# The third unit's down layer as seven products of matrix quarters

## The chip, the cores and the metric

The kernel runs on one core of one Trainium2 chip. A core has five engines that the text names by the profile's short names: PE (TensorE, matrix products), DVE (VectorE), ACT (ScalarE), POOL (GpSimd) and SP (SyncE, which here only issues transfers). Each engine works through its own list of instructions in order and waits on semaphores for the others. The metric is the device time of one execution in microseconds (us), lower is better. The kernel before was timed at 528.81 us (median of three runs, 528.71 to 529.97).

## The reference

Three stages stand one behind the other: a Nystrom attention over 4 batches of 576 tokens, a dense layer with a gated activation, and a routed layer with 8 experts. Only the last one matters here. For the tokens of one expert it computes

```
h = np.maximum(np.einsum('ecd,edf->ecf', disp, w1), 0.0)
y = np.einsum('ecf,efd->ecd', h, w2)
...
out[i] = gate_w[i] * y[expert_idx[i], pos[i]]
```

with D = 512 features, F = 1024 hidden features, everything in float32. The first product with its ReLU is called the up layer here, the second one with the factor gate_w the down layer.

## The kernel before

The last stage is worked off in *units* of 576 tokens of one expert. For the data at hand each of the batches 0 to 2 is one unit, and `run_unit(i)` (L1181) is called three times; the third is the last work of the program. A float32 product is made of three products of a rounded half and a rest: every operand X is split (`split`, L1051) into hi = round(X), written by ACT, and lo = X - hi, written by DVE or POOL, and PE adds hi*hi + hi*lo + lo*hi in one PSUM bank.

Up layer of the second and third unit (`up_seven`, L1137): the product is already done with seven products of matrix quarters instead of eight (the Winograd form of Strassen's method). For each of four blocks m of 128 hidden features PE makes seven products of 6 matmuls of 288 columns; DVE adds them up from PSUM into the buffers `mix` (lines L1140), and `put_h` (L1077) writes ReLU of the four sums: ACT writes hT[0] (hi, L1079) and the last 64 tokens unsplit to `h_tail` (L1081), DVE writes hT[1] (lo, L1082). The PSUM banks of these products form a ring of six. `split2(f)` (L1074) splits the eight 512-wide slices of w2 on ACT and POOL.

Down layer (`down_layer`, L1155): one call for each tile of 128 tokens. The unit has four full tiles and one of 64 tokens. The loop in `run_unit` begins with the small one (16 matmul passes of L1170 in plain float32, its sum and scale at L1176 to L1178), then come the tiles 3, 2, 1, 0. A full tile is 24 matmuls of 512 columns into one bank (8 slices f of the hidden features, three products each, L1163). ACT scales the finished bank with the gate (L1174) and the tile, 256 KB, is stored by a transfer that SP issues (L1197); the last tile's transfer is issued by ACT.

While unit 0 and 1 are in their down layer, ACT and DVE prepare the quarters and their sums for the next unit's up layer (`prepare_w`, `prepare_x`). The third unit has no successor: in its down layer DVE and ACT have little to do. At the end each engine takes a branch (L1365) past a part of the program that is not needed for this data, and the engines meet (L1442). `redo` (L1200) loads the flag for that branch into registers. Instructions of this part of the program are put in order by a scheduler when the kernel is built, so an engine's list is not the order of the source text.

## Time and profile before

| what | us |
|---|---|
| median of three runs | 528.81 |
| the profiled execution | 529.06 |
| its span, first to last instruction | 527.3 |
| third unit: up layer on PE | 474.32 to 497.0 |
| third unit: 64-token tile on PE | 497.03 to 500.6 |
| third unit: four full tiles on PE | 500.62 to 522.67 |
| last scaling on ACT | 522.75 to 523.44 |
| last store issued | 523.47 |

All times inside the program are counted from the start of the span. A row of the timeline gives the start, the length, the engine, the line, what is written from what, the shape, and after x the number of instructions that follow each other without a gap; its length is from the first start to the last end. Ends of matmuls are modelled. The profiled execution took 1.8 us more than its span and 0.25 us more than the median of the runs.

### The profile page before, as it was taken

How to read it: one execution, taken by the hardware profiler on the slowest of the kernel's cores; microseconds unless marked ns; L12 is line 12 of the kernel's file. 1: busy time of each engine (PE TensorE's matmuls, PEld its weight loads, DVE VectorE, ACT ScalarE, POOL GpSimd, SP SyncE). 2: the span in 40 equal slices, each digit the busy share in tenths (PEclk: the TensorE clock that was granted, in tenths of full speed). 3: DMA queues.
4: the chain of work that ended last, by engine and by line, in shares of the span. 5: the costliest groups of instructions: out<-in, count | busy, mean ns of one | idle time of the engine just before them, and what ended most of it. 6: DMA issues, size and time to landing. Idle time of an engine off the chain costs nothing. (4 is left out here: it accounts for less than half of the span.)

```text
span 527.3 us, 12038 instructions
## 1 busy us (share of the span) xinstructions
PE 515.0 (98%) x4760; PEld 449.2 (85%) x4760; DVE 343.0 (65%) x781; ACT 293.9 (56%) x684; POOL 200.7 (38%) x254
## 2 busy tenths in 40 slices
PE   8898899999999999999999999999999999999996
PEld 6565778988889998988989999999897899689785
DVE  0789988656867876854965353357836958987700
ACT  1868878766867554744644343446346564864411
POOL 2468978987230542212513323323160070016000
PEclk9999999999999999999999999999999999999999
DMA  7896803002735521140120000129621470510011
GB/s 272 307 368 231 283 19 99 30 1 91 229 103 154 177 81 35 48 171 1 45 88 0 1 2 1 67 89 322 253 112 56 159 283 1 179 51 23 2 51 44
DMA packets 24240, 59.72 MB, mean 113 GB/s; under 512 B 2928, under 2 KB 7536, under 8 KB 24176
## 3 DMA queue, kind: packets, MB, share of 16 engines
q1 hardware_dynamic: 23360, 58.60, 31.9%
q8 instruction: 39, 0.64, 0.5%
q10 hardware_dynamic: 816, 0.28, 0.2%
q14 instruction: 25, 0.20, 0.1%
HBM read 45.89 MB, written 12.98 MB: 112 GB/s over the span
## 5 line engine op out<-in xcount | busy, mean ns | idle before, releaser
L433 PE MATMUL py<-ghi,wo 128*128 128x288 f32 x768 | 157.7, 297 | 0.0
L419 POOL TENSOR_TENSOR glo<-r,ghi 128x288 fp32r<-128x288 f32 x88 | 74.5, 849 | 137.7 <-ACT ghi L412 80.3
L433 PEld LDWEIGHTS py<-ghi,wo 128*128 128x128 f32 x768 | 123.2, 188 | 2.6 <-issue 2.0
L389 PE MATMUL ph<-at,vv 128*128 128x288 f32 x768 | 121.6, 299 | 1.0 <-DVE r L402 0.7
L389 PEld LDWEIGHTS ph<-at,vv 128*128 128x128 f32 x768 | 106.6, 188 | 11.2 <-issue 4.3
L433 PE MATMUL py<-glo,wo 128*128 128x288 f32 x384 | 113.5, 296 | 0.0
L400 ACT ACTIVATE r<-ph,half 128x288 f32<-128x288 f32 x128 | 63.5, 500 | 62.3 <-PE ph L389 33.7
L402 DVE SCALAR_TENSOR_TENSOR r<-r,ph 128x288 f32<-128x288 f32 x128 | 56.9, 450 | 48.8 <-ACT r L400 47.9
L433 PEld LDWEIGHTS py<-glo,wo 128*128 128x128 f32 x384 | 72.1, 188 | 0.0
L1163 PE MATMUL ps_o<-w2s,hT 128*128 128x512 f32 x288 | 66.2, 390 | 0.0
L1163 PEld LDWEIGHTS ps_o<-w2s,hT 128*128 128x128 f32 x288 | 53.8, 188 | 13.5 <-issue 2.4
L1053 POOL TENSOR_TENSOR w2s<-wi,w2s 128x512 fp32r<-128x512 f32 x24 | 31.6, 1344 | 87.0 <-ACT w2s L1052 87.0
L412 ACT ACTIVATE ghi<-r 128x288 fp32r<-128x288 f32 x96 | 42.1, 444 | 33.5 <-DVE r L402 33.3
L445 DVE TENSOR_TENSOR yacc<-py,yacc 128x288 f32<-128x288 f32 x72 | 32.7, 454 | 33.9 <-PE py L433 33.8
L1140 DVE TENSOR_TENSOR mix<-ps,mix 128x288 f32<-128x288 f32 x56 | 23.9, 452 | 11.6 <-PE ps L1132 10.9
L276 POOL TENSOR_TENSOR wo<-cvt,wo 128x512 fp32r<-128x512 f32 x16 | 21.0, 1313 | 24.3 <-ACT wo L274 18.9
L1079 ACT ACTIVATE hT<-mix 128x288 fp32r<-128x288 f32 x32 | 13.7, 445 | 26.8 <-DVE mix L1140 26.8
L369 DVE TENSOR_TENSOR vv<-ps_v,vv 128x512 fp32r<-128x512 f32 x32 | 21.8, 686 | 7.0 <-ACT vv L367 6.8
L735 PE MATMUL pn<-yy 128*128 128x96 f32 (+2 forms) x112 | 22.3, 293 | 2.2 <-POOL yy L687 1.5
L735 PEld LDWEIGHTS pn<-yy 128*128 128x128 f32 x112 | 17.1, 189 | 8.0 <-POOL yy L687 2.6
L1174 ACT ACTIVATE rows_o<-ps_o,prob 128x512 f32<-128x512 f32 x12 | 8.3, 689 | 24.0 <-PE ps_o L1163 19.2
L367 ACT ACTIVATE vv<-ps_v 128x512 fp32r<-128x512 f32 x32 | 18.4, 593 | 4.0 <-PE ps_v L362 3.9
(219 smaller groups left out, 831.3 us busy)
## 6 DMA issues: line engine op xcount, KB each, us to landing
raw<-in_moe_w_in SPq DMA_DIRECT2D x16, 512.0 KB, 4.0
raw<-in_moe_w_out SPq DMA_DIRECT2D x16, 512.0 KB, 4.6
wi<-in_moe_w SPq DMA_DIRECT2D x6, 1024.0 KB, 6.5
r_d<-r SPq DMA_DIRECT2D x32, 144.0 KB, 1.9
vm<-in_v SPq DMA_DIRECT2D x8, 512.0 KB, 7.2
raw<-in_moe_w SPq DMA_DIRECT2D x4, 1024.0 KB, 6.3
qT<-in_q SPq DMA_DIRECT2D x6, 576.0 KB, 6.0
qT<-in_k SPq DMA_DIRECT2D x6, 576.0 KB, 7.3
```

The lines of the kernel that those rows point to most:

```text
L369: nc.vector.tensor_tensor(lo[:, b, :], ps[i], hi[:, b, :].bitcast(F32), op=ALU.subtract)
L389: nc.tensor.matmul(ph, lhsT=vv[pair][g][a][:, b, f * P:(f + 1) * P], rhs=at[pair][c][:, g, tok], start=n == 0, stop=n == 3 * NG - 1)
L400: nc.scalar.activation(r, ph, AF.Relu, bias=half, scale=1.0 / 6.0)
L402: nc.vector.scalar_tensor_tensor(r, r, 1.0, ph, op0=ALU.min, op1=ALU.mult)
L412: nc.scalar.activation(ghi, r, AF.Copy)
L419: nc.gpsimd.tensor_tensor(glo, r, ghi.bitcast(F32), op=ALU.subtract)
L433: nc.tensor.matmul(py, lhsT=w[a][:, f, d * P:(d + 1) * P], rhs=gh[f][c], start=f == 0 and n == 0, stop=f == NF - 1 and n == 2)
L445: nc.vector.tensor_tensor(y, py, y, op=ALU.add)
L735: nc.tensor.matmul(pn[:, cols], lhsT=yy[:, 0:P], rhs=yy[:, cols], start=True, stop=True)
L1053: engine.tensor_tensor(dst[1], src, dst[0].bitcast(F32), op=ALU.subtract)
L1140: plus = lambda dst, ps, x: nc.vector.tensor_tensor(dst, ps, x, op=ALU.add)
L1163: nc.tensor.matmul(ps, lhsT=hT[a][:, f, cols], rhs=w2s[c][:, f, :], start=n == 0, stop=n == 3 * FC - 1)
```

## The change

The four full tiles of the third unit, a product of 512 tokens x 1024 by 1024 x 512, are no longer done tile by tile. A new function `down_seven` makes them with the seven products of quarters: with A = h (tokens by hidden features) and B = w2 cut into quarters, A11 B11, A12 B21, S1 T1, S2 T2, S3 T3, S4 B22 and A22 T4, where S1 to S4 and T1 to T4 are sums and differences of quarters. Each quarter product is 256 tokens x 512 x 256, done for two blocks m of 128 tokens: 12 matmuls of 256 columns each.

- `put_h` gets `keep`: in the third unit ACT also writes ReLU(h) unsplit to `h32` (the buffers raw1, free by then), 288 or 224 columns at a time, because the sums S are made from it.
- `sums_before`: POOL makes T1 = B12 - B11 and T2 = B22 - T1, each 128 x 1024.
- In `down_seven` DVE makes S1 to S4, T3 and T4 (128 x 1024 each) and the lo parts of all eight sums, ACT their hi parts; DVE adds the products from PSUM; ACT scales with the gate. A11, A12, A22, B11, B21, B22 use the split parts that exist anyway.
- Rows 0 to 127 and 128 to 255 of the unit are stored whole, rows 256 to 511 in a right and a left half (128 KB each). The very last half is scaled and added by DVE in one instruction and stored by ACT's queue. `flag` is the old code for `redo`, called at another place.

The core of the diff (line numbers of the changed file differ by 4 in the middle of the program, by about 100 at its end):

```
-        def put_h(f, hf, x):
+        def put_h(f, hf, x, keep=False):
...
+            if keep:
+                n = min(HB, full - hf * HB)
+                nc.scalar.activation(h32[f // NF][:, f % NF, hf * HB:hf * HB + n], x[:, 0:n], AF.Relu)
...
+        def sums_before():
+            (b11, b12), (b21, b22) = quarters(*raw2)
+            nc.gpsimd.tensor_tensor(early_sums[0], b12, b11, op=ALU.subtract)
+            nc.gpsimd.tensor_tensor(early_sums[1], b22, early_sums[0], op=ALU.subtract)
...
+        def down_seven(i, put, flag):
...
+            where = dict(S1=a22, T1=t1, S2=a11, T2=t2, S3=a21, T3=b12, S4=a12, T4=b21)
+            sums = dict(S1=(a21, a22, ALU.add), S3=(a11, a21, ALU.subtract), S2=(a22, a11, ALU.subtract),
+                        S4=(a12, a11, ALU.subtract), T3=(b22, b12, ALU.subtract), T4=(b21, t2, ALU.subtract))
...
+            def times(a, b, m, ps):
+                n = 0
+                for f in range(NF):
+                    for x, y in ((0, 0), (0, 1), (1, 0)):
+                        nc.tensor.matmul(ps, lhsT=ops[a][x][:, f, m * P:(m + 1) * P], rhs=ops[b][y][:, f, :],
+                                         start=n == 0, stop=n == 3 * NF - 1)
+                        n += 1
+                return ps
...
+            add("S1")
+            parts_of("S1", "T1")
+            add("S3", "S2")
+            for m in pair:
+                copy(y[m], times("A11", "B11", m, new()))
+            parts_of("S2")
+            for m in pair:
+                plus(v[m], times("A12", "B21", m, new()), y[m])
+                copy(row[m][:, left], v[m], scale=gates[m])
+            parts_of("T2")
+            add("S4", "T3")
+            for m in pair:
+                plus(w[m], times("S1", "T1", m, new()), y[m])
+            parts_of("S3", "T3")
+            add("T4")
+            for m in pair:
+                ps = times("S2", "T2", m, new())
+                plus(u[m], ps, y[m])
+                plus(v[m], ps, w[m])
+            flag()
+            parts_of("S4")
+            for m in pair:
+                ps = times("S3", "T3", m, new())
+                plus(w[m], ps, v[m])
+                plus(u[m], ps, u[m])
+                copy(row[m + 2][:, right], w[m], scale=gates[m + 2])
+                copy(u[m], u[m], scale=gates[m + 2])
+                put(m + 2, row[m + 2], nc.sync, right)
+            parts_of("T4")
+            for m in pair:
+                plus(v[m], times("S4", "B22", m, new()), v[m])
+                copy(row[m][:, right], v[m], scale=gates[m])
+                put(m, row[m], nc.sync)
+            for m in pair:
+                nc.vector.scalar_tensor_tensor(row[m + 2][:, left], times("A22", "T4", m, new()), gates[m + 2], u[m],
+                                               op0=ALU.mult, op1=ALU.add)
+                put(m + 2, row[m + 2], nc.scalar if m else nc.sync, left)
...
-                    hi = up_seven(f)
+                    hi = up_seven(f, not more)
...
+                if not more and f == NF - 1:
+                    sums_before()
...
+                if not more:
+                    down_seven(i, lambda k, ro, engine, c=slice(0, DM): engine.dma_start(out[i * S + k * P:i * S + (k + 1) * P, c], ro[:, c]), flag)
+                    return
```

DVE's list from the last sums of the up layer on, before. The names: mix are the up layer's sums, hT_5659 the lo part of h, rows_o the output of the 64-token tile.

```order
L1140 TENSOR_TENSOR mix_5674<-ps_6821,mix_5674 128x288
L1140 TENSOR_TENSOR mix_5673<-ps_6831,mix_5673 128x288
L1082 SCALAR_TENSOR_TENSOR hT_5659<-mix_5674,hT_5658 128x288
L1082 SCALAR_TENSOR_TENSOR hT_5659<-mix_5673,hT_5658 128x288
L1177 TENSOR_TENSOR rows_o_5662<-ps_o,rows_o_5662 64x512
L1365 COMPARE_AND_BRANCH
```

And the same place in the changed program. Here w1s_5665 is the lo part of T1, raw_5678 (written) S1, wo_119 the lo part of T2, w1s_5664 that of S1, raw_5677 S3 and then S2; mix_5672 <- ps_d is the first sum of a product of the down layer (A12 B21 for m = 0).

```order
L1144 TENSOR_TENSOR mix_5674<-ps_6835,mix_5674 128x288
L1144 TENSOR_TENSOR mix_5673<-ps_6846,mix_5673 128x288
L1054 TENSOR_TENSOR w1s_5665<-rx,w1s_5665 128x4x256
L1083 SCALAR_TENSOR_TENSOR hT_5659<-mix_5674,hT_5658 128x288
L1083 SCALAR_TENSOR_TENSOR hT_5659<-mix_5673,hT_5658 128x288
L1215 TENSOR_TENSOR raw_5678<-raw_5677,raw_5678 128x4x256
L1054 TENSOR_TENSOR wo_119<-rx,wo_119 128x4x256
L1181 TENSOR_TENSOR rows_o_5662<-ps_o,rows_o_5662 64x512
L1054 TENSOR_TENSOR w1s_5664<-raw_5678,w1s_5664 128x4x256
L1215 TENSOR_TENSOR raw_5677<-raw_5677 128x4x256
L1237 TENSOR_TENSOR mix_5672<-ps_d,mix_5669 128x256
L1215 TENSOR_TENSOR raw_5677<-raw_5678,raw_5677 128x4x256
```

DVE's list, which ended behind the 64-token tile, now goes on with 14 instructions of 1024 elements (one of them already ahead of the last two lo parts of h) and 16 of 256. Behind S2 (raw_5677) the order is: the sum of m = 1, S4, lo of S2, T3, two sums, lo of S3, lo of T3, T4, four sums, lo of S4 (w1s_5667), four sums, lo of T4 (vv_124), two sums, and the two last instructions, which scale and add.

PE's list in the changed program, from the third of the seven products on. Here w1s_5665 and w1s_5664 are T1 and S1, wo_119 and w1s_5666 T2 and S2, at_117 and at_118 the hi and lo of T3, wo_120 is S3, w1s_5667 S4, w2s B22.

```order
L1225 MATMUL ps_d<-w1s_5665,w1s_5664 128x256 x24
L1225 MATMUL ps_d<-wo_119,w1s_5666 128x256 x24
L1280 TENSOR_LOAD redo
L1225 MATMUL ps_d<-at_117,wo_120 128x256 x2
L1225 MATMUL ps_d<-w2s_5656,w1s_5667 128x256
L1225 MATMUL ps_d<-w2s_5657,w1s_5667 128x256
L1225 MATMUL ps_d<-w2s_5656,w1s_5667 128x256
L1225 MATMUL ps_d<-w2s_5657,w1s_5667 128x256
L1225 MATMUL ps_d<-at_118,wo_120 128x256
```

Before, 96 matmuls of 128x512 from w2s and hT stood here. Behind these rows follow 21 more of S3 T3, 2 of A22 T4 (vv_123, the hi part of T4), 20 of S4 B22 that begin with the lo part of S4, and 22 of A22 T4 that begin with the lo part of T4 (vv_124).

## Rows read from the trace of the kernel before

**Rows 1.** Page, part 1: busy time, share of the span, instructions.

```profile
PE 515.0 (98%) x4760; PEld 449.2 (85%) x4760; DVE 343.0 (65%) x781; ACT 293.9 (56%) x684; POOL 200.7 (38%) x254
```

**Rows 2.** Third unit's up and down layer: length, busy us (x) by engine, PEclk, DMA.

```profile
474.30:497.00 22.70, 22.70 (x170) 22.50 (x168) 18.02 (x40) 9.97 (x29) 9.00 (x7) 1.00 0.04 14
...
500.60:522.70 22.10, 22.07 (x98) 17.94 (x96) 0.68 (x1) 3.40 (x5) 0.00 (x0) 1.00 0.12 43
```

**Rows 3.** Timeline of the down layer's full tiles and of the end.

```profile
500.62 22.05 PE L1163 MATMUL ps_o<-w2s,hT 128*128 128x512 f32 x96
...
506.39 0.69 ACT L1174 ACTIVATE rows_o<-ps_o,prob 128x512 f32<-128x512 f32 x1 [3.58 <-PE ps_o L1163]
511.83 0.69 ACT L1174 ACTIVATE rows_o<-ps_o,prob 128x512 f32<-128x512 f32 x1 [4.75 <-PE ps_o L1163]
...
522.75 0.69 ACT L1174 ACTIVATE rows_o<-ps_o,prob 128x512 f32<-128x512 f32 x1 [4.75 <-PEq L1365]
523.47 0.37 ACTq L1197 DMA_DIRECT2D out<-rows_o  x1
```

**Rows 4.** Timeline, PE: two neighbouring products of the third up layer.

```profile
485.74 0.96 PE L1132 MATMUL ps<-xw,w1s 128*128 128x288 f32 x6
...
486.54 0.96 PE L1132 MATMUL ps<-at,vv 128*128 128x288 f32 x6
```

**Rows 5.** Timeline, PE: warming matmuls early in the program.

```profile
11.35 0.83 PE L984 MATMUL warm<-ident 128*128 128x256 bf16 x6
```

**Rows 6.** Timeline, DVE: back to back, while the third unit is prepared.

```profile
460.90 1.22 DVE L1112 TENSOR_TENSOR raw<-raw,raw 128x1024 f32<-128x1024 f32 x1
462.03 0.76 DVE L1125 TENSOR_TENSOR w1s<-rx,xw 128x576 fp32r<-128x576 f32 x1
```

**Rows 7.** Timeline, DVE sums from PSUM: four in a row, then two.

```profile
489.00 1.75 DVE L1140 TENSOR_TENSOR mix<-ps,mix 128x288 f32<-128x288 f32 x4
...
492.01 0.82 DVE L1140 TENSOR_TENSOR mix<-ps,mix 128x288 f32<-128x288 f32 x2
```

**Rows 8.** Timeline: the end of the third up layer and the 64-token tile.

```profile
497.01 0.82 DVE L1140 TENSOR_TENSOR mix<-ps,mix 128x288 f32<-128x288 f32 x2
...
497.03 3.65 PE L1170 MATMUL ps_o<-wi,h_tail 128*64 128x512 f32 x16
497.50 0.81 ACT L1079 ACTIVATE hT<-mix 128x288 fp32r<-128x288 f32 x2 [0.87 <-DVE mix L1140]
...
497.98 0.83 DVE L1082 SCALAR_TENSOR_TENSOR hT<-mix,hT 128x288 fp32r<-128x288 f32 x2
...
501.36 0.68 DVE L1177 TENSOR_TENSOR rows_o<-ps_o,rows_o 64x512 f32<-64x512 f32 x1 [2.56 <-ACT rows_o L1176]
```

**Rows 9.** Timeline, ACT: two hi parts of 1024 elements in a row.

```profile
450.40 1.99 ACT L1052 ACTIVATE w1s<-raw 128x1024 fp32r<-128x1024 f32 x2
```

**Rows 10.** Timeline: POOL's last lo parts of w2, a DVE instruction beside them.

```profile
475.29 8.01 POOL L1053 TENSOR_TENSOR w2s<-wi,w2s 128x512 fp32r<-128x512 f32 x6
...
479.11 1.55 DVE L1082 SCALAR_TENSOR_TENSOR hT<-mix,hT 128x288 fp32r<-128x288 f32 x1
```

**Rows 11.** Transfers from 450 us on: count, KB each, median us to landing.

```profile
out<-rows_o SPq DMA_DIRECT2D x7, 256.0 KB, 2.0
out<-rows_o SPq DMA_DIRECT2D x2, 128.0 KB, 3.1
```

**Rows 12.** Events of the branch L1365 by queue: ns, first to last start in us.

```profile
L1365 SPq EVENT_SEMAPHORE  x9: 17/17/17, 518.9 to 525.6; - x9
...
L1365 DVEq EVENT_SEMAPHORE  x2: 21/21/21, 504.3 to 504.4; - x2
...
L1365 DVEq COMPARE_BRANCH  x1: 72/72/72, 501.4 to 501.4; - x1
```

**Rows 13.** Events of the engines' meeting L1442: SP's, in the same form.

```profile
L1442 SPq DRAIN  x3: 7/7/13, 526.4 to 526.7; - x3
```

**Rows 14.** Where the flag for the branch is loaded: PE's queue.

```profile
L1200 PEldq TENSOR_LOAD <-redo x1: 726/726/726, 507.6 to 507.6; - x1
```

More of the change, by code (lines that the diff above doesn't have):

```diff
@@ L1135, in product, with up_seven @@
             return ps
-        def up_seven(m):
+        def up_seven(m, keep=False):
             u, v, w, y = mix[m % 2]
@@ L1148, in up_seven @@
             plus(u, ps, u)
-            put_h(m + NF, 1, w)
+            put_h(m + NF, 1, w, keep)
             plus(v, product("A22", "T4", m), v)
-            put_h(m + NF, 0, v)
+            put_h(m + NF, 0, v, keep)
             plus(u, product("S4", "B22", m), u)
-            return put_h(m, 1, u)
+            return put_h(m, 1, u, keep)
         def down_layer(t, gate, put):
@@ L1179, in down_layer @@
             put(ro[0:r, :])
+        h32 = [t.rearrange("p a (b n) -> p (a b) n", n=full) for t in raw1]
+        early_sums = [rx[:, i * NF * P * 2:(i + 1) * NF * P * 2].rearrange("p (f n) -> p f n", f=NF) for i in range(2)]
+        places = [t[:, :, i * 2 * P:(i + 1) * 2 * P] for t in (*w1t[0], w1t[1][0], *wo[0]) for i in range(2)]
+        places += [t.rearrange("p a b -> p (a b)")[:, 0:NF * 2 * P].rearrange("p (f n) -> p f n", f=NF) for t in at[0]]
+        w1d = w1t[1][1]
+        places += [w1d[:, :, i * 2 * P:(i + 1) * 2 * P] for i in range(2)]
@@ new lines, in nystrom_moe_kernel, with add, parts_of @@
+        places += [vv[0][0][a].rearrange("p a b -> p (a b)").rearrange("p (f n) -> p f n", f=NF) for a in range(2)]
+        def sums_before():
[3 more added lines that the diff above has]
+        def down_seven(i, put, flag):
+            (a11, a21), (a12, a22) = quarters(*h32)
+            (b11, b12), (b21, b22) = quarters(*raw2)
+            t1, t2 = early_sums
+            where = dict(S1=a22, T1=t1, S2=a11, T2=t2, S3=a21, T3=b12, S4=a12, T4=b21)
+            sums = dict(S1=(a21, a22, ALU.add), S3=(a11, a21, ALU.subtract), S2=(a22, a11, ALU.subtract),
+                        S4=(a12, a11, ALU.subtract), T3=(b22, b12, ALU.subtract), T4=(b21, t2, ALU.subtract))
+            ops = {name: places[2 * n:2 * n + 2] for n, name in enumerate(where)}
+            half_ = lambda ts, k, c: [t[:, k * NF:(k + 1) * NF, c * 2 * P:(c + 1) * 2 * P] for t in ts]
+            ops.update(A11=half_(hT, 0, 0), A12=half_(hT, 1, 0), A22=half_(hT, 1, 1),
+                       B11=half_(w2s, 0, 0), B21=half_(w2s, 1, 0), B22=half_(w2s, 1, 1))
+            def add(*names):
+                for name in names:
+                    x, y, f = sums[name]
+                    nc.vector.tensor_tensor(where[name], x, y, op=f)
+            def parts_of(*names):
+                for name in names:
+                    split(ops[name], where[name], nc.vector)
+            def times(a, b, m, ps):
[6 more added lines that the diff above has]
+                return ps
+            new = lambda: bank([P, 2 * P], "ps_d")
+            gates = [prob[:, i, t, :] for t in range(4)]
+            row = [rx[:, 2 * NF * 2 * P:2 * NF * 2 * P + DM], *rows_o]
+            row = [row[1], row[3], row[0], h_rows]
+            left, right = slice(0, 2 * P), slice(2 * P, 4 * P)
+            y, u, w, v = ([mix[m][j][:, 0:2 * P] for m in range(2)] for j in range(4))
+            copy = lambda dst, ps, **kw: nc.scalar.activation(dst, ps, AF.Copy, **kw)
+            plus = lambda dst, ps, x: nc.vector.tensor_tensor(dst, ps, x, op=ALU.add)
+            pair = range(2)
+            add("S1")
[35 more added lines that the diff above has]
+                put(m + 2, row[m + 2], nc.scalar if m else nc.sync, left)
@@ L1181, in run_unit, with flag @@
+        def flag():
+            tc.mark_branch_hint_location("again", engines=(ET.SP, ET.Activation))
+            state["again"] = nc.values_load_multi_w_load_instructions(
+                redo, min_val=0, max_val=1, skip_runtime_bounds_check_because=ON_CHIP, bass_reorder=False)[1][0]
         def run_unit(i):
@@ L1195, in run_unit @@
                 rows = slice(i * S + k * P, i * S + k * P + size(k))
-                last = not more and t == NST - 1
-                down_layer(k, prob[0:size(k), i, k, :], lambda ro: (nc.scalar if last else nc.sync).dma_start(out[rows, :], ro))
-                if not more and t == NST - 3:
-                    tc.mark_branch_hint_location("again", engines=(ET.SP, ET.Activation))
-                    state["again"] = nc.values_load_multi_w_load_instructions(
-                        redo, min_val=0, max_val=1, skip_runtime_bounds_check_because=ON_CHIP, bass_reorder=False)[1][0]
+                down_layer(k, prob[0:size(k), i, k, :], lambda ro: nc.sync.dma_start(out[rows, :], ro))
+                if not more:
+                    down_seven(i, lambda k, ro, engine, c=slice(0, DM): engine.dma_start(out[i * S + k * P:i * S + (k + 1) * P, c], ro[:, c]), flag)
+                    return
                 if more and t == 0:
```

3 lines of the change are left out of this document (2 added, 1 removed).

## Prediction

> **What bounds the kernel now.** Read first the page's busy times [rows 1]: PE is busy 515.0 of 527.3 us, the other engines at most 65%. Next the stretches of the third unit [rows 2]: in both layers PE is busy all the time at the full granted clock, and in the down layer DVE works 0.68 and ACT 3.40 us of 22.10. The timeline [rows 3] shows what an end looks like: 96 matmuls without a gap from 500.62 to 522.67, ACT's scaling until 523.44, the store issued at 523.47. Nothing stands beside this chain, so whatever ends the last scaling earlier ends the program earlier. One full tile takes 511.83 - 506.39 = 5.44 us, 227 ns for a matmul of 512 columns.
>
> **PE: removed and added.** Removed: 96 x 0.227 = 21.8 us. Added: 7 products x 2 blocks x 12 = 168 matmuls of 256 columns, a form that does not stand in this trace with these operands. Neighbouring products of the up layer start 0.80 us apart [rows 4], 133 ns for 288 columns. A straight line through 288 columns (133) and 512 (227) has 0.42 ns per column and gives 120 ns for 256. The bounds: 133 ns from above, the row of 288 columns itself; from below the warming matmuls of 256 bf16 columns [rows 5], (0.83 - 0.27)/5 = 111 ns, 0.27 being about the length of one. I take 120, next to the nearer row. Then PE needs 168 x 0.120 = 20.2 us: one eighth of the columns is saved, 2.7 us of 21.8, and 1.1 us is lost again because each matmul carries about 13 ns beside its columns and there are 72 more of them. The saving on PE is 1.6 us, if it never waits.
>
> [...]
>
> **DVE: the new chain.** Added are 14 instructions of 1024 elements (six sums, eight lo parts) and 16 of 256. Back to back, one of 1024 elements starts 462.03 - 460.90 = 1.13 us before the next, though it is 1.22 long [rows 6]; one of 288 elements 0.82 - 0.45 = 0.37 [rows 7]. The line through both gives 0.34 for 256 elements (0.42 long). So 14 x 1.13 + 16 x 0.34 = 21.3 us of DVE work come into a stretch of 22 us where it was idle: DVE, not PE, becomes the tight engine, and the sum has to follow its list in order.
>
> The start [rows 8]: the last two sums of the up layer start at 497.01 and end their turn at 497.75. The lo part of T1 now stands before the last two lo parts of h: 498.88, then 499.62. S1 needs the last kept copy of h from ACT. ACT was free for the last two hi parts at 497.50; with the two kept copies and the tail between them (0.36, 0.36, 0.36, 0.15 and 0.39) it is ready at 499.1, in time. S1 and the lo part of T2 take DVE to 501.88, the 64-token tile's addition (0.68, 0.60 until the next) to 502.47, the lo part of S1 and S3 to 504.73. Here DVE waits: the next is the sum of A12 B21, and PE, which starts at 500.62 as before, has done 36 matmuls at 500.62 + 35 x 0.120 + 0.28 = 505.10. From 505.13 on nothing makes DVE wait: the hi parts that it needs come from ACT, which takes about 1.0 us for one [rows 9] and is given each at least one DVE instruction ahead. Seven instructions of 1024 elements and eight of 256 later, at 515.76, starts the lo part of S4, done at 516.98; four sums later, at 518.25, that of T4, done at 519.47.
>
> PE meets this twice. Behind the lo part of S4 it has 20 matmuls, to 519.4. Behind the lo part of T4 it has 22: the last starts at 519.50 + 21 x 0.120 = 522.02, its result is there at 522.30, and the last DVE instruction (0.42) ends at 522.75. Before it was 523.44. So 0.7 us are gained at the last sum, 0.9 less than PE alone saves, because the matmuls behind the last lo part stand on the path.
>
> **The end.** The last store is 128 KB in place of 256 KB. A 256 KB store lands after 2.0 us, the two of 128 KB after 3.1, but one of those shared the queues with the loads of w2 [rows 11]. Bounds: a gain of 1.0 us, if the whole landing time went with the bytes, and a loss of 1.1 us by the other row. I take a gain of 0.2, near the 256 KB row, since no load runs at that time. The four stores ahead of it are issued at least 1.4 us (12 matmuls) earlier. DVE now reaches its branch last: before, it branched at 501.4 and had its next event 2.9 us later [rows 12]. Branching at 522.4 gives 525.3. SP waits for the landing until 525.6 now and drains at 526.4 [rows 13], 0.9 earlier in the forecast, 525.5. So the branch is covered by 0.2 us; without that cover it costs no more than the 0.2 us that the shorter store gives.
>
> **What is hidden.** In the up layer ACT gets 16 kept copies (about 0.36 each) and two hi parts of 1.0: 7.8 us beside 9.97 busy of 22.70 [rows 2]. The copy of each next first product now stands behind the kept copies, some 0.8 us late; PE has a ring of six banks, 4.8 us of products, and does not notice. If it did, it would cost up to 0.8 us per block, 2.4 in all. POOL's two sums of 1024 elements take about 2.6 us each, twice its 1.3 us for 512 [rows 10]; its last lo part of w2 then ends at 488 or 489, and PE asks for it from 500.6 on. A DVE instruction with both inputs in SBUF stretches beside POOL (1.55 us in place of 0.45), so DVE may lose up to 2.6 us twice, before the up layer and in its first block; the ring, and the five products that stand before the first use of T4 of the up layer, cover that. PE's load of the flag took 0.73 us at 507.6 [rows 14], within the tile of 5.44 us above, and costs nothing in the middle of a stream.
>
> Sum: 0.7 + 0.2 = 0.9 us. The profiled execution took 529.06, so 528.2; the median of the runs is 0.25 lower, so 527.9.
>
> **Rivals.** First, DVE doesn't overlap its instructions (slower). Where an instruction waits for the one before, the early start is gone: four dependent sums in a row take (1.75 - 0.45)/3 = 0.43 each [rows 7]. If the whole list went so (1.22 for 1024 elements, 0.43 for 256, 0.45 for 288), S3 would end at 505.59, the lo part of T4 would be ready at 505.59 + 8 x 1.22 + 12 x 0.43 + 1.22 = 521.73, and the last sum would end 3.28 later, at 525.01: 1.6 later than before, with the shorter store 1.4, 530.2. It is slower as soon as the list from 497 on grows by more than 0.9 us. For it: nearly each of these instructions waits for another engine. Against it: so do those of [rows 6], and they overlap.
>
> [...]
>
> Second, PE is the bound (faster): DVE keeps ahead, by a quicker form or by waits that are shorter than I count. Then the last result comes at 500.62 + 167 x 0.120 + 0.28 = 520.94, the end at 521.39, 2.05 earlier, with the store 2.25: 526.6. For it: DVE's list misses this by only 1.4 us. Against it: 30 instructions, all with durations from rows.
>
> Third, the matmuls of 256 columns take as long as those of 288: PE alone ends at 500.62 + 167 x 0.133 + 0.29 = 523.1, with the waits for S4 and T4 at 523.2, the last sum at 523.6: nothing gained but the store, 528.8. For it: the load of 128 weights before each matmul is the same and may set the pace. Against it: from 512 to 288 columns the pace followed the columns.
>
> **How the numbers follow.** A measurement of this kernel tells 0.3% from no change, 1.6 us: below 527.2 is faster, above 530.4 slower. The forecast gets 0.50 (its own range 527.3 to 528.6), DVE without overlap 0.15, PE as the bound 0.20, no saving on PE 0.15. Faster: nearly all of the second rival and a little of the forecast's edge, 0.23. Slower: less than half of the first and 0.05 for a mishap that I don't see, 0.11. Within 0.3%: 0.66. The range of 526.4 to 530.1 leaves out the lowest part of the second rival and half of the first.
>
> **What would show it.** Right: matmuls of 256 columns 120 ns apart; DVE nearly without idle time from 498 to 519.5; PE idle in short gaps before the lo parts of T3, S4 or T4, 1 to 1.5 us together; the last DVE instruction's end near 522.7; the last store landing within 2.0 us. Wrong: a PE pace of 111 or 133 ns; DVE instructions of 1024 elements 1.22 apart; a PE gap in the up layer; an end that waits for DVE's branch. Gaps of PE of more than 3 us would break the forecast.

## The result: 0.5% slower

The changed kernel took 531.83 us (median of 8 runs, 531.12 to 533.35), the kernel before beside it 528.88 (8 runs): the ratio of the means is 1.0051, 95% interval 1.0035 to 1.0066. The forecast was 527.9 us, a gain too small to be told from no change; its range ended at 530.1. The profiled execution took 531.69 us, its span is 530.0 us. One execution of e8 below took 2791 us, a slow one, and is left out of its row.

Not all of that belongs to the change. The first thing to look at is where the two traces part. The stretches of the changed kernel, with the granted clock behind the engines' busy times (the kernel before has 1.00 in both):

```profile
40.00:60.00 20.00, 16.70 (x222) 11.32 (x222) 18.44 (x48) 16.72 (x46) 17.29 (x31) 0.93 0.73 242
60.00:90.00 30.00, 30.00 (x484) 24.60 (x483) 25.32 (x66) 24.11 (x68) 23.15 (x30) 0.99 0.30 100
```

The granted clock is a share of full speed: it was 0.52 from 57 to 60 us, 0.74 from 60 to 61, and 1.00 in the rest of the two stretches. This dip lies 400 us ahead of the first changed instruction, and what stands behind it comes about 1 us late: PE's first matmul of the third up layer starts at 475.50, before at 474.55 (the 474.32 in the table of the kernel before is the start of its weight load). Of the runs below, e7 dips in the same stretch (0.90) and e12 and e13 do not (1.00); the third up layer starts at 475.30 to 476.97 in e4, e6, e7, e8 and e10 and at 474.10 to 474.83 in the others. The program there is unchanged, so I take the dip for chance; that is argued, not shown. The mean clock of a whole execution doesn't tell it, because it also counts the time behind PE's last matmul, where the clock falls (in e12 0.56 from 525 to 526 us and 0.50 from there on): e17 has a mean of 0.996, though its up layer starts at 474.25. So from here on times are counted **from the start of the third up layer on PE**, behind which the clock is 1.00 in every trace (474 to 522 us). Counted so, the span of the changed kernel ends after 54.50 us, before after 52.75: in these two traces 1.75 us are the change's own.

The kernel before at the place where the two part, DVE and PE:

```profile
466.97 0.76 DVE L1125 TENSOR_TENSOR at<-rx,at 128x576 fp32r<-128x576 f32 x1
467.64 1.22 DVE L1112 TENSOR_TENSOR raw<-raw,raw 128x1024 f32<-128x1024 f32 x1
...
474.55 0.96 PE L1132 MATMUL ps<-xw,w1s 128*128 128x288 f32 x6
...
476.41 0.46 DVE L1140 TENSOR_TENSOR mix<-ps,mix 128x288 f32<-128x288 f32 x1 [3.49 <-PE ps L1132]
```

DVE of the changed kernel in the preparation and in the up layer (start, length, what; an x with a number: that many without a gap; in brackets the idle time before and who ended it):

```profile
466.80 1.22 DVE L1054 TENSOR_TENSOR w1s<-raw,w1s 128x1024 fp32r<-128x1024 f32 x1
467.93 2.95 DVE L1129 TENSOR_TENSOR at<-rx,at 128x576 fp32r<-128x576 f32 x1
470.81 1.21 DVE L1116 TENSOR_TENSOR raw<-raw,raw 128x1024 f32<-128x1024 f32 x1
...
478.74 1.75 DVE L1144 TENSOR_TENSOR mix<-ps,mix 128x288 f32<-128x288 f32 x4 [3.46 <-ACT mix L1145]
...
491.63 1.75 DVE L1144 TENSOR_TENSOR mix<-ps,mix 128x288 f32<-128x288 f32 x4 [0.26 <-ACT mix L1145]
...
496.99 1.75 DVE L1144 TENSOR_TENSOR mix<-ps,mix 128x288 f32<-128x288 f32 x4 [0.26 <-ACT mix L1145]
...
499.99 0.81 DVE L1144 TENSOR_TENSOR mix<-ps,mix 128x288 f32<-128x288 f32 x2
500.73 1.22 DVE L1054 TENSOR_TENSOR w1s<-rx,w1s 128x1024 fp32r<-128x1024 f32 x1
501.86 0.82 DVE L1083 SCALAR_TENSOR_TENSOR hT<-mix,hT 128x288 fp32r<-128x288 f32 x2
502.59 1.22 DVE L1215 TENSOR_TENSOR raw<-raw,raw 128x1024 f32<-128x1024 f32 x1
```

POOL and ACT beside it:

```profile
466.96 3.31 POOL L1196 TENSOR_TENSOR rx<-wi 128x1024 f32<-128x1024 f32 x1 [32.41 <-DVE at L1129]
474.80 2.90 POOL L1054 TENSOR_TENSOR w2s<-wi,w2s 128x512 fp32r<-128x512 f32 x2 [4.53 <-ACT w2s L1053]
477.66 2.39 POOL L1197 TENSOR_TENSOR rx<-wi,rx 128x1024 f32<-128x1024 f32 x1
```

```profile
474.11 3.74 ACT L1053 ACTIVATE w2s<-wi 128x512 fp32r<-128x512 f32 x7
477.75 0.67 ACT L1178 ACTIVATE rows_o<-ps_o,prob 128x512 f32<-128x512 f32 x1
478.32 0.39 ACT L1145 ACTIVATE mix<-ps 128x288 f32<-128x288 f32 x1
...
490.93 0.38 ACT L1087 ACTIVATE raw<-mix 128x224 f32<-128x224 f32 x1
491.21 0.39 ACT L1145 ACTIVATE mix<-ps 128x288 f32<-128x288 f32 x1
...
501.49 0.24 ACT L1082 ACTIVATE h_tail<-mix 128x64 f32<-128x64 f32 x1
```

The lo part at 467.93 takes 2.95 us instead of 0.75: it ends 0.6 us behind POOL's first sum, which the scheduler had put ahead of the low parts of w2. From there the delay walks on: the last sum for the up layer (470.81, before 467.64), its hi part on ACT, the seven hi parts of w2 behind that (474.11), the first copy of a product (478.32). DVE's first sums come 478.74 - 475.50 = 3.24 us behind the layer's start, before 1.86. The last two come at 24.49 in place of 22.46 (497.01 in [rows 8]), and S1, the head of the down layer's chain, at 27.09 in place of the 25.07 of the forecast.

PE, the first product of the up layer and from the layer's end on:

```profile
475.50 0.96 PE L1136 MATMUL ps<-xw,w1s 128*128 128x288 f32 x6
...
501.79 1.08 PE L1174 MATMUL ps_o<-wi,h_tail 128*64 128x512 f32 x4 [0.75 <-ACT h_tail L1082]
502.79 6.02 PE L1225 MATMUL ps_d<-w2s,hT 128*128 128x256 f32 x48
508.65 3.04 PE L1225 MATMUL ps_d<-w1s,w1s 128*128 128x256 f32 x24
511.53 3.29 PE L1225 MATMUL ps_d<-wo,w1s 128*128 128x256 f32 x24
...
515.99 2.89 PE L1225 MATMUL ps_d<-at,wo 128*128 128x256 f32 x22 [0.46 <-DVE at L1054]
...
519.59 2.65 PE L1225 MATMUL ps_d<-w2s,w1s 128*128 128x256 f32 x20 [0.46 <-DVE w1s L1054]
522.07 2.85 PE L1225 MATMUL ps_d<-vv,hT 128*128 128x256 f32 x22
```

The 64-token tile waits 0.75 us for its last quarter, the rows that ACT writes to `h_tail` at 501.49, and so the down layer starts 27.29 us behind the up layer's start, not 26.07 [rows 3]. In it PE does what was forecast: 48 matmuls in 6.02 us, 24 in 3.04, 0.12 us each, and it waits for DVE's lo parts at S2 T2, S3 T3 and S4 B22. It takes 22.13 us, as long as the 96 wide matmuls before, 22.05.

The end: DVE's last lo part and its last instruction, the last store, and the events of the branch by queue (ns, first to last start):

```profile
520.79 1.20 DVE L1054 TENSOR_TENSOR vv<-wi,vv 128x1024 fp32r<-128x1024 f32 x1
...
525.05 0.48 DVE L1273 SCALAR_TENSOR_TENSOR wi<-ps_d,prob,mix 128x256 f32<-128x256 f32 x1 [0.82 <-PE ps_d L1225]
```

```profile
out<-wi ACTq DMA_DIRECT2D x1, 128.0 KB, 2.2
```

```profile
L1467 SPq EVENT_SEMAPHORE  x9: 17/17/17, 525.7 to 528.3; - x9
...
L1467 DVEq EVENT_SEMAPHORE  x2: 21/21/21, 528.1 to 528.2; - x2
...
L1467 DVEq COMPARE_BRANCH  x1: 72/72/72, 525.1 to 525.1; - x1
```

The store issued at 525.56 lands 2.2 us later, and DVE's events at 528.2 come just ahead of SP's last one. From the last matmul to the end of the span it takes 5.08 us, before 4.63. The difference lies behind the landing: from there to the end it is 2.21 us, before 1.77. SP's nine events of the branch are its waits for the transfers, in the same order in both traces and 0.07 to 0.08 us apart behind the last landing. The changed kernel's last store is the second of the nine, and seven more follow its landing (527.78 to 528.28); before, it was the eighth, and one followed (525.50 to 525.57).

### The profile page after: what moved, and what is told of

Same layout as the page of the kernel before. It is cut to its first block, busy times and chain, and to the rows that moved or that the text cites. A ratio compares the mean times of both kernels' runs of the same rounds, so it can differ in the third digit from the quotient of the medians.

```text
span 530.0 us, 12264 instructions
## 1 busy us (share of the span) xinstructions
PE 515.6 (97%) x4832; PEld 452.3 (85%) x4832; DVE 367.4 (69%) x811; ACT 307.7 (58%) x714; POOL 206.5 (39%) x256
## 4 chain that ended last, share of the span: by engine, by line
PE 85%; DVE 10%; ACT 3%; issue 1%; DMA 0%; POOL 0%; ACTq 0%; DVEq 0%; POOLq 0%
PE py L433 27%; PE ph L389 18%; PE ps L1136 8%; PE ps_o L1167 8%; PE ps_h L1098 5%; PE ps_v L362 3%; PE pn L735 3%; PE warm L984 1%; PE ps_o L1174 1%; PE ps_f L537 1%; PE ps_w L299 1%; PE ps_d L1225 1%; PE pb L578 1%; PE pw L715 1%; DVE w1s L1054 1%
## 5 line engine op out<-in xcount | busy, mean ns | idle before, releaser
L1167 PE MATMUL ps_o<-w2s,hT 128*128 128x512 f32 x192 | 44.1, 390 | 0.0
L1167 PEld LDWEIGHTS ps_o<-w2s,hT 128*128 128x128 f32 x192 | 35.9, 188 | 9.0 <-issue 1.6
L1083 DVE SCALAR_TENSOR_TENSOR hT<-mix,hT 128x288 fp32r<-128x288 f32 x32 | 18.8, 592 | 2.8 <-ACT hT L1080 0.9
```

The costliest lines, as they stand in the source:

```text
L1167: nc.tensor.matmul(ps, lhsT=hT[a][:, f, cols], rhs=w2s[c][:, f, :], start=n == 0, stop=n == 3 * FC - 1)
```

## The experiments

What each run gave. First and last sums: when DVE starts the up layer's first and last two sums; start: when the down layer starts on PE; all three from the start of the third up layer on PE. Down: the down layer on PE. End: from its last matmul to the end of the span. Ratio: of the means, to the kernel before on the same chip (medians of the latter 529.72 for e1 to e4, 529.84 for e5 to e8, 529.65 for e9 to e12, 528.92 for e13 to e16, 528.96 for e17 and e18).

| kernel | first sums | last sums | start | down | end | us, median | ratio, 95% interval |
|---|---|---|---|---|---|---|---|
| before | 1.86 | 22.46 | 26.07 | 22.05 | 4.63 | 528.88 | 1 |
| changed | 3.24 | 24.49 | 27.29 | 22.13 | 5.08 | 531.83 | 1.0051 [1.0035, 1.0066] |
| e1 late sums | 1.86 | 25.87 | 28.67 | 22.15 | 5.30 | 532.47 | 1.0060 [1.0040, 1.0079] |
| e2 copies later | 3.24 | 23.82 | 26.62 | 22.14 | 5.63 | 530.49 | 1.0020 [1.0006, 1.0034] |
| e3 hint for DVE | 3.24 | 24.47 | 27.27 | 22.13 | 5.38 | 531.27 | 1.0037 [1.0023, 1.0052] |
| e4 all three | 1.86 | 25.51 | 28.32 | 22.15 | 5.83 | 532.62 | 1.0054 [1.0034, 1.0073] |
| e5 sums on DVE | 3.41 | 24.56 | 27.36 | 22.15 | 4.97 | 532.01 | 1.0040 [1.0027, 1.0053] |
| e6 e5 and e2 | 3.42 | 23.89 | 26.69 | 22.15 | 5.35 | 531.16 | 1.0032 [1.0018, 1.0045] |
| e7 left halves early | 3.24 | 24.47 | 27.27 | 22.16 | 5.50 | 530.78 | 1.0025 [1.0014, 1.0036] |
| e8 e6, e7 and e3 | 3.41 | 23.89 | 26.70 | 22.16 | 5.52 | 531.20 | 1.0019 [1.0004, 1.0034] |
| e9 no sums | 1.86 | 23.87 | 26.67 | 22.15 | 5.36 | 530.57 | 1.0026 [1.0015, 1.0037] |
| e10 no kept copies | 3.23 | 23.79 | 26.29 | 22.46 | 5.32 | 530.58 | 1.0018 [1.0006, 1.0030] |
| e11 whole stores | 3.24 | 24.47 | 27.27 | 22.16 | 5.54 | 531.27 | 1.0034 [1.0020, 1.0049] |
| e12 other order of matmuls | 3.24 | 24.47 | 27.27 | 20.78 | 5.87 | 530.43 | 1.0020 [1.0010, 1.0030] |
| e13 neither sums nor copies | 1.87 | 22.85 | 26.07 | 21.91 | 5.40 | 530.24 | 1.0019 [1.0008, 1.0031] |
| e14 e12 and e2 | 3.24 | 23.81 | 26.61 | 20.78 | 6.56 | 529.86 | 1.0022 [1.0010, 1.0035] |
| e15 e14, two queues | 3.24 | 23.80 | 26.60 | 20.77 | 5.51 | 529.44 | 1.0008 [0.9997, 1.0020] |
| e16 e15 and e7 | 3.23 | 23.80 | 26.60 | 20.78 | 5.42 | 529.18 | 1.0008 [0.9997, 1.0020] |
| e17 e16 and e3 | 3.24 | 23.80 | 26.60 | 20.77 | 5.68 | 529.24 | 1.0006 [0.9992, 1.0020] |
| e18 e17, sums in pieces | 3.23 | 23.22 | 26.07 | 20.72 | 5.58 | 528.49 | 0.9995 [0.9985, 1.0005] |

The columns of the trace up to Down repeat to 0.03 us where nothing that they depend on was changed. End does not: in the changed kernel, e1 to e6, e9, e10 and e13, whose stores are the same, it goes from 4.97 to 5.83, because the last landing goes from 2.12 to 2.98. The medians carry the clock too: two kernels whose traces differ by 0.2 us can lie 1 us apart in them, and ratios that differ by less than their intervals decide nothing here.

**First group: POOL's sums (A), the kept copies (B), DVE's branch (C; e3 gives the hint for the branch, which SP and ACT have, to DVE too).**

```
e1
-                if not more and f == NF - 1:
-                    sums_before()
+                if not more and f == FC - 1:
+                    with tc.issue_after(lo.ins):    # POOL's last lo part of w2
+                        sums_before()
e2
-            nc.scalar.activation(y, product("A11", "B11", m), AF.Copy)
+            first = nc.scalar.activation(y, product("A11", "B11", m), AF.Copy)
+            with tc.issue_after(first.ins):
+                keep_now()                          # the kept copies of block m - 1
e3
-            tc.mark_branch_hint_location("again", engines=(ET.SP, ET.Activation))
+            tc.mark_branch_hint_location("again", engines=(ET.SP, ET.Activation, ET.DVE))
e4: e1, e2 and e3
```

> The two sums of quarters on POOL stand behind its last low part of the down matrix, instead of among the low parts; nothing is left out. Theory A (POOL's first sum, 3.31 us from 466.96 in the changed kernel, holds DVE's preparation of the third unit, and its second the small sums): DVE's low part beside it falls from 2.95 to about 0.8 us, the first copy of a product on ACT comes some 1.5 us earlier, the sum S1 of the down layer 1.5 to 2 us earlier, and the time falls to 529.8 to 530.4. Theory B (the sixteen kept copies on ACT are the cause): the down layer gains at most 0.4 us, 531.4 to 531.9. Theory D (only a chance dip of the clock earlier): 531.5 to 532.

A missed. The preparation is as it was before (first sums at 1.86), yet the last sums come later still. DVE and POOL of e1:

```profile
482.65 3.18 DVE L1083 SCALAR_TENSOR_TENSOR hT<-mix,hT 128x288 fp32r<-128x288 f32 x2
485.76 1.74 DVE L1144 TENSOR_TENSOR mix<-ps,mix 128x288 f32<-128x288 f32 x4
```

```profile
482.90 2.62 POOL L1196 TENSOR_TENSOR rx<-wi 128x1024 f32<-128x1024 f32 x1
485.60 2.50 POOL L1197 TENSOR_TENSOR rx<-wi,rx 128x1024 f32<-128x1024 f32 x1
```

Two small operations that took 1.09 us together in the kernel before now take 3.18, until POOL's first sum has ended. The hold moved with the sum. The four sums at 485.76, one input from PSUM, run beside POOL's second sum in 1.74 as ever.

> The kept copies of one block of the hidden rows stand behind ACT's first copy of the next block, not ahead of it; those of the last block stay; POOL's sums stay early; nothing is left out. Theory A: S1 gains 0.3 us at most, 531.4 to 531.9. Theory B: ACT's first copies come 1 us and more earlier, DVE catches up in the up layer, S1 comes 1.5 to 2 us earlier, 529.8 to 530.4. If both have a share, 530.4 to 531.2.

The copies cost: 0.67 us back at the start of the down layer. The rate shows why. DVE takes up block 3 and 4 of the up layer 5.36 us apart in the changed kernel (491.63, 496.99) and 4.97 in e2 (490.06, 495.03), as before. PE needs 5.6 for a block. So the kept copies ahead of ACT's first copy cut what DVE can make good per block from 0.63 to 0.24 us.

> [...] Theory C (DVE's branch, 3.0 us from 525.1 to 528.1, ends last): DVE's events after the last sum come 0.5 us and more earlier, SP's last event then follows the store's landing at 527.8, and the time falls by 0.3 to 0.5, to 531.3 to 531.5. Else (the store's landing ends last, or the hint does nothing on DVE): 531.8 within 0.2.

DVE's events came 0.6 us behind its branch instead of 3.0, and the end of the span stayed 5.4 us behind the last matmul: the store landed after 2.5 us, SP's last event came 0.5 behind that. The branch did not end last; C fell for this kernel.

> All three edits together. If A alone is right, 529.5 to 530.0 with the hint's share; if B alone, the same; if the two shares add, S1 comes where the prediction had it, 2 us earlier than in the changed kernel, and the time is 528.9 to 529.5, or with the clock of the kernel before up to 1 us less, 527.9. If none of the three is right, 531.8.

Nothing of that: the late sums spoil what the moved copies give.

**Second group: the sums where DVE is idle, and the stores (F).**

```
e5 (the call of sums_before also moves ahead of the loop over f)
-            nc.gpsimd.tensor_tensor(early_sums[0], b12, b11, op=ALU.subtract)
-            nc.gpsimd.tensor_tensor(early_sums[1], b22, early_sums[0], op=ALU.subtract)
+            nc.vector.tensor_tensor(early_sums[0], b12, b11, op=ALU.subtract)
+            nc.vector.tensor_tensor(early_sums[1], b22, early_sums[0], op=ALU.subtract)
e6: e5 and e2
e7
                 copy(row[m][:, left], v[m], scale=gates[m])
+                put(m, row[m], nc.sync, left)
...
-                put(m, row[m], nc.sync)
+                put(m, row[m], nc.sync, right)
e8: e2, e3, e5 and e7
```

> The two sums of quarters run on DVE (some 1.2 us each) in its idle 3.5 us ahead of the third up layer's first sums; POOL does none; nothing is left out. From the start of the third up layer on PE to that of its down layer the kernel before took 26.07 us and the changed one 27.29. Theory A2 (DVE's operations with two inputs in SBUF stand still until a POOL operation that runs is through, so that POOL's first sum costs DVE 2.2 us wherever it is put, and the kept copies on ACT keep DVE from making it good): 26.1 to 26.5, S1 some 1.5 us earlier than in the changed kernel, the two waits of 0.46 in the down layer smaller, 530.0 to 530.8. Theory B2 (the kept copies alone): 27.0 to 27.3, 531.3 to 531.9. Theory E (DVE has no room at all): 27.5 and more, 532 and more.

> The sums on DVE and the kept copies behind the next block's first copy; nothing is left out. A2: the two shares add, from the up layer to the down layer 26.07 to 26.2 as in the kernel before, S1 where the prediction had it (25.1 us behind the start of the up layer, in the changed kernel 27.1), the down layer's two waits of 0.46 us gone and its products in 20.7 to 21.4 us (now 22.13), 528.9 to 529.7. B2: as with the kept copies moved alone, 26.6 and 530.5.

A2 missed in both: DVE has 3.5 us of idle time there, but POOL, free of its sums, began the low parts of w2 at 471.46 already, and DVE's second sum took 2.20 us beside them. First sums at 3.41. Moved copies again gave 0.67.

> The changed kernel with the left halves of its first two tiles stored as soon as they are there (about 511), and only their right halves at 522.9, so that 512 KB and not 768 KB are issued in the last 4 us; nothing is left out. Theory F (the stores crowd the end: the last half lands in 2.2 to 3.0 us, the kernel before's whole tile in 2.0): the last landing takes 2.0 or less, from the last matmul to the end of the span 4.7 and less instead of 5.1 to 5.8, 531.2 to 531.5. Else: 531.8 within 0.2.

The trace refutes F as a matter of bytes: with 256 KB less at the end, the stores there landed after 3.5, 3.8 and 2.8 us, and the end took 5.50. The lower median is not explained by the trace; the intervals of the two ratios still touch (1.0036 and 1.0035).

> All together: sums on DVE, kept copies behind the next first copy, left halves stored early, hint for DVE; nothing is left out. A2 with F: 528.2 to 529.2, at or below the kernel before of the same chip. If the down layer stays at 22.1 us because DVE's chain, not its start, sets it: 529.3 to 530. If nothing adds: 530.5.

e8 is e6 in its up layer and e7 in its end; nothing added beyond that.

**Third group: each suspect left out, and the order on PE (G).**

```
e9
-                if not more and f == NF - 1:
-                    sums_before()
e10 (DVE's sums of h are tied to their old places in its list)
-                    hi = up_seven(f, not more)
+                    hi = up_seven(f)
e11
-                put(m + 2, row[m + 2], nc.sync, right)
...
-                put(m + 2, row[m + 2], nc.scalar if m else nc.sync, left)
+                put(m + 2, row[m + 2], nc.scalar if m else nc.sync)
e12 (terms: (0, 0) first, the one with the later lo part last; was f, then terms, for each m by itself)
+                for x, y in terms:
+                    for m in pair:
+                        for f in range(NF):
+                            nc.tensor.matmul(pss[m], lhsT=ops[a][x][:, f, m * P:(m + 1) * P], rhs=ops[b][y][:, f, :],
```

> The two sums of quarters are left out (their places are read as they are), nothing takes their place; the kept copies stay. In the changed kernel DVE's last two sums of the up layer begin 24.49 us behind the layer's start on PE, in the kernel before 22.46. Theory A3 (both shares are needed: the sums hold DVE up by some 2 us, and the kept copies make the ring between ACT and DVE 5.36 us per block in place of 4.97, so that against PE's 5.60 it cannot make good what it lost): without the sums nothing is lost, 22.5 to 23.2, from the up layer's start to the down layer's 26.1 to 26.4, 1 us less than in the changed kernel. If the kept copies are the whole cause: 24 and more, as in the changed kernel. If the sums cost nothing wherever they stand, likewise.

> The sixteen kept copies are left out (the sums of quarters of h are made of what stands in their places, at the same points of DVE's order); POOL's sums stay early. A3: the first sums still come 3.24 us behind the layer's start, but the ring makes good 0.6 us per block: the last two begin at 22.5 to 23.2, the down layer at 26.1 to 26.5, 0.8 to 1.2 us less than in the changed kernel. If POOL's sums alone are the cause: 24 and more, as in the changed kernel.

Either alone gives 0.6 to 1.0 us of the 1.22 at the start of the down layer. At the last matmul (start and down together) it is 0.60 and 0.67, since PE in e10, early, then waits longer for DVE. The last sums came later than A3 had them (23.87 and 23.79): in e9 the ring between ACT and DVE is still at 5.35 us per block and DVE's operations beside POOL's low parts are as long as before (1.55 and 1.18 us at 479.09 and 480.93, there 1.55 and 1.18); in e10 it is at 4.97, but the first sums start 1.38 late.

> The last two tiles are stored whole, 256 KB each, behind the last operations on them, not in halves; nothing is left out. If the halves cost (more stores in flight, longer landings): the last landing takes 2.0 us as in the kernel before, 0.2 to 0.5 less than in the changed kernel. If the halves gain: the last landing takes 3.3 us, as the whole tiles did at 522.9, and the end comes 0.5 to 1.1 us later. If neither: within 0.2.

Neither gain nor cost on this scale: the last whole store landed after 3.1 us, the end took 5.54. Two things cancel here: the landing is longer, but the stretch behind it is 1.77 us and not 2.21, as before the change, likely because with two stores less SP's wait for the last one is the eighth of nine again.

> In the down layer PE does a product's matmuls for both blocks of rows side by side, those that need the low part which DVE makes last at the end; the same matmuls, nothing is left out; up layer and stores as in the changed kernel. Theory G (in the second half PE waits for DVE's low parts, and the 22 matmuls behind the last of them stand on the path): the two waits of 0.46 us and the slow product S2 T2 go, 8 matmuls (1.0 us) stand behind the last low part instead of 22, and the down layer takes 20.5 to 21.2 us instead of 22.13: 530.2 to 530.8 where the changed kernel has 531.8. If DVE's own chain only shifts with the products: 21.8 to 22.2 and no change.

G held. PE of e12 in the down layer:

```profile
507.39 3.04 PE L1227 MATMUL ps_d<-w1s,w1s 128*128 128x256 f32 x24
510.27 3.04 PE L1227 MATMUL ps_d<-wo,w1s 128*128 128x256 f32 x24
513.15 3.04 PE L1227 MATMUL ps_d<-at,wo 128*128 128x256 f32 x24
516.03 2.08 PE L1227 MATMUL ps_d<-w2s,w1s 128*128 128x256 f32 x16
...
518.35 1.22 PE L1227 MATMUL ps_d<-w2s,w1s 128*128 128x256 f32 x8
519.41 2.92 PE L1227 MATMUL ps_d<-vv,hT 128*128 128x256 f32 x23
```

S1 T1, S2 T2 and S3 T3 take 3.04 us each, and of the waits for DVE one of some 0.3 us is left (before the lo part of S4, 518.35): 20.78 us in place of 22.13. So PE's waits were a matter of order: the lo part that DVE made last stood in every third matmul from the first on. 0.8 of the 1.35 us were lost again behind the last matmul, where now more stores stand closer together; some of that can be the spread of End.

**Fourth and fifth group: both suspects out, and what ends the program.**

```
e13: e9 and e10. e14: e2 and e12
e15: e14 and
-                put(m + 2, row[m + 2], nc.sync, right)
+                put(m + 2, row[m + 2], nc.scalar if m else nc.sync, right)
...
-                put(m, row[m], nc.sync)
+                put(m, row[m], nc.scalar if m else nc.sync)
e16: e15 and e7. e17: e16 and e3
e18: e17 and (the second sum likewise)
-            nc.gpsimd.tensor_tensor(early_sums[0], b12, b11, op=ALU.subtract)
+            for f in range(NF):
+                nc.gpsimd.tensor_tensor(early_sums[0][:, f, :], b12[:, f, :], b11[:, f, :], op=ALU.subtract)
```

> Both the two sums on POOL and the sixteen kept copies are left out (what is made of them is made of what stands in their places, at the same points of DVE's order). A3: DVE's first sums 1.86 us behind the up layer's start and its last two at 22.4 to 22.7, as in the kernel before; from the up layer's start to the down layer's 26.07 to 26.2. If a third cause exists (the low part of T1 in the up layer, the hi parts on ACT): 26.4 and more.

This is nearly the forecast's up layer. DVE and PE of e13, whose up layer starts at 474.12, 0.43 ahead of the kernel before:

```profile
475.99 0.46 DVE L1144 TENSOR_TENSOR mix<-ps,mix 128x288 f32<-128x288 f32 x1 [3.49 <-PE ps L1136]
...
496.97 0.82 DVE L1144 TENSOR_TENSOR mix<-ps,mix 128x288 f32<-128x288 f32 x2
...
499.57 1.22 DVE L1215 TENSOR_TENSOR raw<-raw,raw 128x1024 f32<-128x1024 f32 x1
...
522.22 0.48 DVE L1276 SCALAR_TENSOR_TENSOR wi<-ps_d,prob,mix 128x256 f32<-128x256 f32 x1 [0.83 <-PE ps_d L1225]
```

```profile
496.61 3.65 PE L1174 MATMUL ps_o<-wi,h_tail 128*64 128x512 f32 x16
500.19 6.01 PE L1225 MATMUL ps_d<-w2s,hT 128*128 128x256 f32 x48
```

With 0.43 added: last two sums at 497.40 (forecast 497.01), S1 at 500.00 (499.62), the down layer at 500.62 (500.62), the last DVE instruction done at 523.13 (522.75). For the start of the down layer the two suspects are the whole 1.22 us. For DVE they are not quite: its last two sums still come at 22.85 and not at 22.46, more than expected (22.7), because ACT's hi parts of T1 and T2, 1.04 us each, now stand among its parts of h and DVE waits for them once (0.60 us). What remains wrong is that 0.4 us and the end: 5.40 us.

> The reordered products of the down layer and the kept copies behind the next block's first copy; nothing is left out. The two gains add if they stand one behind the other on the path: up layer 26.62 as with the copies moved alone, down layer 20.8 as with the order alone, behind the last matmul 5.4 to 5.9: 529.2 to 529.9, the kernel before within 0.1%. If DVE's chain sets the down layer's end whatever PE does: 529.9 to 530.5.

> As the kernel with both edits, and of the last six stores three go to ACT's queue and three to SP's (before one and five); nothing is left out. If the long landings come of many stores on one queue: SP's issues go back from 0.8 to 1.4 us to 0.34, the last landing from 2.2 to 3.1 us to 2.0 to 2.3, 0.5 to 0.8 us less than with one queue. If the transfers themselves are the limit (DMA busy 0.98 of a microsecond at 380 GB/s): no change within 0.2.

> As that, and the left halves of the first two tiles stored at once when they are there, 12 us ahead; nothing is left out. If bytes in flight count: 0.3 to 0.5 us less again, 528.6 to 529.3, below the kernel before of the same chip by 0.1 to 0.2%. If the number of stores at the end counts (six in either): no change.

The gains of e12 and e2 add on PE, but e14 gives 1 us of them away at the end (6.56): SP takes 1.61 us to issue two stores. With three of six stores on ACT's queue an issue takes 0.33 to 0.90 us, and the end is 5.51. The last two landings stay long (3.5 and 2.7 us), with 256 KB less as well (2.9 and 2.7), and e16 is no faster than e15 (1.0008 both): issuing was one part, the landings the other, and what sets those I can't say.

> The kernel with reordered products, moved kept copies, shared and early stores, and the branch hint for DVE too; nothing is left out. Theory C2 (now that the stores land earlier, DVE's branch ends last): SP's last event follows the landing, 0.2 to 0.4 us earlier, 0.1% below the kernel before of the same chip. If the landing ends last all the same: as without the hint, level with the kernel before.

No change again: SP's last event came at 525.6, by the landing (522.26 + 3.0).

> As that, and POOL's two sums of 1024 elements in four pieces of 256 each; nothing is left out. If DVE's operation with two inputs in SBUF stands still until the POOL operation that runs is through: the low part beside POOL's first sum takes 0.8 to 1.5 us instead of 2.95, the first sums of the up layer come 1.9 to 2.6 us behind its start instead of 3.24, and the down layer starts 26.1 to 26.4 behind it instead of 26.60; 0.2 to 0.5 us less than with whole sums. If POOL and DVE share by the byte: 2.95 again and no change.

Half a hit. DVE and POOL of e18 in the preparation:

```profile
466.13 1.76 DVE L1054 TENSOR_TENSOR w1s<-raw,w1s 128x1024 fp32r<-128x1024 f32 x1
467.81 1.29 DVE L1136 TENSOR_TENSOR at<-rx,at 128x576 fp32r<-128x576 f32 x1
469.02 1.76 DVE L1123 TENSOR_TENSOR raw<-raw,raw 128x1024 f32<-128x1024 f32 x1
470.70 1.30 DVE L1136 TENSOR_TENSOR w1s<-rx,w1s 128x576 fp32r<-128x576 f32 x1
```

```profile
465.67 5.71 POOL L1210 TENSOR_TENSOR rx<-wi 128x256 f32<-128x256 f32 x4 [31.80 <-DVE rx L1133]
```

Four DVE operations now lose 0.55 us each where one lost 2.2: the same sum, so the first sums are no earlier (3.23). The gain is in the up layer, where the first small operations take 0.58 and 0.62 us and not 0.99 and 1.18 (e17): the down layer starts at 26.07. This version is level with the kernel before, 0.9995 [0.9985, 1.0005], 0.6% below the changed kernel's ratio; that it beats the kernel before is not shown.

## Why the prediction was wrong

**The step that failed is "What is hidden".** It had both suspects with about the right prices (a kept copy 0.36, a hold of up to 2.6 us twice, ACT's first copies 0.8 us late) and set their sum to nothing, because PE's ring of six banks covers them. In the up layer PE was covered: its products run on with gaps of 0.1 us. But the down layer's chain starts on DVE, not on PE, and PE's 64-token tile needs `h_tail`, which ACT writes behind DVE's last sums. The chain's start was read off the trace of before [rows 8], from a DVE that had caught up with PE; the step asked only whether PE would notice, not when DVE would be free. What the runs showed: POOL's sum puts DVE 1.4 us back ahead of the layer, the kept copies take away the speed with which DVE makes good such delays, and S1 starts at 27.09 in place of 25.07. Against e13, which has neither, the copies alone cost 1.02 us at the last sums (e9), POOL's sums alone 0.94 (e10), both 1.64. That is less than the two added: that one suspect makes the other worse is not shown. The prediction named its own limit, "slower as soon as the list from 497 on grows by more than 0.9 us"; the list did not grow, it started 2.0 us later.

**The end was mis-sized.** Forecast from the last matmul's result to the end of the span: 4.1 us, with 0.2 gained by the smaller store. Measured: 5.08 in the changed kernel, 5.0 to 6.6 in the others. Of the 0.98 in the changed kernel about 0.15 lie ahead of the store's issue, 0.40 in the landing (2.20 for 1.8) and 0.44 behind it, in SP's order of waits, which the prediction took over unchanged from the kernel before. The 3.1 us row of [rows 11] was set aside because loads ran beside it; here other stores of the same kernel did: six are issued from 520.4 to 525.6, where the kernel before issues one. That these stores lengthen the landing is likely, not shown.

So counted from the up layer's start, the span is 2.65 us longer than forecast: 1.22 up to the down layer, 0.45 in it, 0.98 behind it. The first two are one thing, DVE's chain: S1 is 2.0 us late, the last lo part 1.6, PE's last matmul 1.7. The dip of the clock adds 0.95.

**What was right.** The pace of 0.120 us per matmul; DVE overlapping its instructions, S1 to the last lo part's start in 520.79 - 502.59 = 18.20 us (forecast 18.63); the waits before the lo parts and the 22 matmuls behind the last; no rival of the three happened. That the branch would be covered held as well, with nothing to spare (528.2 against 528.3). The saving on PE, 1.6 us if it never waits, was there to be had: e12 shows 1.3 of it. Two small figures of its sum are off without effect: by its own slope the columns save 2.6 us and the 72 more matmuls cost 0.9 (it has 2.7 and 1.1), and the lower bound of the pace is 112 ns, not 111.

## What to carry to other kernels

When a change adds a chain on an engine that was nearly idle, its start is set by when that engine is free of the stage before; recompute that time with everything the change adds to that stage, also where the matrix engine has cover. Added work on a second engine can cost without being long, by slowing the loop in which a late engine catches up: sixteen copies of some 0.4 us took the pace from 4.97 to 5.36 us per block, and DVE came out 1.0 us later. The order in which the last engine waits for the transfers belongs to the end of a program: here it was 0.44 us. And where a low part is ready last, put the matmuls that need it last: that alone was worth 1.35 us on PE here, though 0.8 of it went again at the end.

## What was not expected of the hardware

- Beside a POOL operation a DVE operation with two inputs in SBUF took longer. The lo part at 467.93 took 2.95 us instead of 0.75, 2.20 more, where 2.34 were left of POOL's sum of 3.31; in e1 two small ones took 3.18 instead of 1.09 beside a sum of 2.62, in e18 four took some 0.55 more each beside four pieces. The one at 466.80, under way when POOL started at 466.96, took 1.22, as it does alone. e1's four additions with one input in PSUM took 1.74 beside POOL's second sum, 1.75 with POOL idle (491.69). That DVE stands still until POOL's operation ends is my reading of these lengths; the prediction had read the 1.55 us of [rows 10] as a stretching.
- DVE's next event came 2.9 to 3.6 us behind its branch without the hint (3.0 in the changed kernel, 3.6 in e12 and e15), and 0.5 to 0.6 with it (e3, e4, e17, e18).
- Landings grew towards the end of the program: the first two of the last six stores landed after 1.7 to 2.6 us, the ones behind them after 2.1 (e5) to 4.0 (e11, two stores in the median), with 128 KB (e7: 3.5 and 3.8) as with 256 KB (the changed kernel: 3.3), on one queue or two (e15: 3.5). What limits them stays open.
